# First pair of an attention kernel: one-hot and maximum rows transposed to the operands' own partitions, first head in column thirds, a planner with per-engine latencies

## The chip, the cores and the metric

The kernel runs on one core of one Trainium2 chip. The metric is device microseconds of one execution: before the change the median of three runs is 796.49 us (795.05, 796.49 and 796.76). A change of less than 0.2% (1.6 us) can't be told from none with such a measurement.

## What is computed

Clustered attention, then two feed-forward layers, all in float32:

```python
q_assign = argmax(einsum('bhsd,hcd->bhsc', q_n, c_n))   # k_assign likewise, 16 clusters
mask = q_assign[:, :, :, None] == k_assign[:, :, None, :]
scores = where(mask, scale * q @ k.T, -1e9)
attn = softmax(scores);  x = attn @ v                    # b=2, h=8, s=768, d=64
h = x @ moe_w_in;  x = (max(h,0) + alpha*min(h,0)) @ moe_w_out      # 1536x512, d_ff 2048
h = x @ moe2_w_in; x = (P(h)/Q(h)) @ moe2_w_out          # P cubic, Q from |h| and h*h
```

## The kernel before

**Precision.** Each float32 operand is split into a high part and the rest, and a product is three matmuls (high·high, high·low, low·high). The weights arrive as 64-bit words, and ScalarE, VectorE and GpSimd decode them (L992 to L1012) before a feed-forward step can use them.

**Attention, by pairs of heads.** There are 8 pairs (16 heads), and per pair j these steps: `load` brings q and k (L450); `ph_T` transposes them (L520, L522 for pair 0, L525 for the others) and splits them (L530, L532); `ph_logits` multiplies by the centroids (L552); `ph_lt` transposes the logits (L566) and makes a one-hot row of the best cluster in five VectorE instructions (L574 to L580); `ph_oht` transposes the one-hot of both heads at once (L590) and ScalarE scales it (L594).

**Operands.** `operands1(i)` copies to head i's operand `op1` with DMAs: q and k (L617), the one-hot of k's clusters (L620) and that of q's as 0 or -2^60 (L623). They have to be DMAs, since the rows go to other partitions than those on which they were made. `operands2(i)` copies the low parts to `op2` (L632, L636).

**Scores.** `max_chunk` multiplies `op1` by itself (L664), 9 chunks of 512 columns a head, and VectorE reduces each to row maxima (L670). `m_chain` collects them (L678), transposes them on TensorE (L684), ScalarE negates them (L686), and a DMA puts them as one more row into `op1` (L690). Only then can `st_chunk` make the scores minus the maximum (L709, L710) in 9 chunks; ScalarE takes the exponential (L714), the result is split into 16-bit high and low parts (`p_split`: L414/L416 and L726), and `pv_tile` multiplies by v (L773, L775; L787 to L789). `pv_fin` divides (L804 to L812), and `x_T` transposes for the feed-forward (L826).

**Feed-forward.** 96 steps of 512 columns; each is 12 matmuls of `emit_h` (L1029) and 12 of `emit_y` (L1098), with an activation between that runs on the other engines.

**Warm-up.** 57 operations of two small matmuls each (L848) with a low priority fill TensorE where it has nothing else.

**What sets the order.** All steps are operations of a planner, `Sched`. It has a cost for each operation and engine, keeps a modelled time for each engine, takes the operation that it can start first (weighted by a due time `SC.t`), and at the end writes the instructions of each engine in the order of their modelled starts. So a changed number changes the order on all engines, and the chip then executes each engine's list strictly in that order, with semaphores between them. All transfers stand in one list, SP's. The model of before takes a transfer's bytes at 280 GB/s and one latency of 0.16 us between any two engines:

```python
    LAT = 0.16
...
                moved = max(moved, start + 1.28) + cost
                o.end = moved + 1.05
...
        return n / 280e3
```

## Time and profile before

| what | value |
|---|---|
| median of three runs | 796.49 us |
| the profiled execution | 797.74 us, its span 796.0 us, 1.74 us around it |
| busy share of the span | TensorE 96%, VectorE 75%, ScalarE 70%, GpSimd 73% |
| mean granted clock of TensorE | 0.984 |
| attention, until the first feed-forward matmul | 252.09 us |
| first scores of head 0 (L709) | at 29.88 us |
| dense feed-forward | from about 277 us to 787 us |

The profile's page gives busy times, the chain of waits that ended last, and the costliest groups; the trace answers with a timeline of each engine, the waits of an engine by what released it, and the busy time in chosen windows with the granted clock. "SPq" is the issue of a transfer. A matmul's duration overlaps that of the next, so TensorE's rate is read from the distance of starts, not from durations.

### The profile page before, as it was taken

To read this page: it belongs to the slowest core of one execution; us is meant where nothing else is said; L and a number is where in the kernel's file an instruction comes from. 1 tells how busy PE (TensorE), PEld (TensorE's weight loads), DVE (VectorE), ACT (ScalarE), POOL (GpSimd) and SP (SyncE) were. 2 spreads that over 40 slices of the span, in tenths; PEclk is the share of its full clock that TensorE was granted. 3 is DMA by queue.
4 is the path that set the end of the run, shared out by engine and by line. 5 is a ranking of instruction groups with operands and counts; after the bars stand their busy time and mean duration, and the time that the engine had idled before them with its cause. 6 is when DMAs were issued, how large, how long until landed. Compare 5 with 4: busy or idle time off the path is not lost.

```text
span 796.0 us, 13977 instructions
## 1 busy us (share of the span) xinstructions
PE 765.4 (96%) x5295; PEld 636.0 (80%) x5295; DVE 599.4 (75%) x871; ACT 560.3 (70%) x991; POOL 579.7 (73%) x475
## 2 busy tenths in 40 slices
PE   8998999999997799999999999999999999999996
PEld 7687797887886688888888888888888888888885
DVE  5787787888797999775662563479889899777775
ACT  3377877887878666665653664688899798666672
POOL 4286956967679899996762773799889689667443
PEclk9899999999899999999999999999999999999999
DMA  5685757656442433332320330211112110000012
GB/s 129 127 171 115 156 126 151 136 123 175 97 102 81 159 99 114 107 108 77 107 80 0 106 96 11 79 54 54 53 54 80 53 54 1 0 1 1 1 54 106
DMA packets 57859, 67.58 MB, mean 85 GB/s; under 512 B 27232, under 2 KB 46272, under 8 KB 57792
## 3 DMA queue, kind: packets, MB, share of 16 engines
q1 hardware_dynamic: 57792, 66.69, 31.9%
q8 instruction: 41, 0.67, 0.4%
q14 instruction: 26, 0.21, 0.1%
HBM read 43.04 MB, written 3.15 MB: 58 GB/s over the span
## 4 chain that ended last, share of the span: by engine, by line
PE 84%; DVE 6%; DMA 5%; ACT 2%; POOL 1%; issue 1%; SPq 1%; DVEq 0%; ACTq 0%; POOLq 0%
PE bank L1029 32%; PE bank L1098 32%; PE bank L709 3%; PE bank L664 3%; PE bank L710 3%; DMA arena_r<-arena_r 2%; PE bank L787 2%; PE bank L552 2%; DVE mp L670 2%; PE bank L789 2%; PE bank L788 2%; DMA arena_p<-in_v 2%; PE bank L525 1%; DMA arena_p<-in_k 1%; DVE arena_p L726 1%
## 5 line engine op out<-in xcount | busy, mean ns | idle before, releaser
L1029 PE MATMUL bank<-x,arena_r 128*128 128x512 f32 x1152 | 277.6, 390 | 3.2 <-ACT arena_r L414 1.1
L1098 PE MATMUL bank<-arena_r 128*128 128x512 f32 x1152 | 277.8, 390 | 1.7 <-ACT arena_r L414 1.0
L1029 PEld LDWEIGHTS bank<-x,arena_r 128*128 128x128 f32 x1152 | 215.9, 188 | 48.9 <-POOL arena_r L1012 3.1
L1098 PEld LDWEIGHTS bank<-arena_r 128*128 128x128 f32 x1152 | 215.6, 188 | 48.4 <-ACT arena_r L414 1.4
L1075 POOL TENSOR_TENSOR arena_r<-arena_p,arena_r 128x512 fp32r<-128x512 f32 x96 | 132.9, 1385 | 38.6 <-ACT arena_r L414 19.8
L726 POOL TENSOR_TENSOR arena_p<-arena_p 128x768 f16<-128x768 f32 x66 | 115.3, 1755 | 18.7 <-ACT arena_p L414 15.1
L414 ACT CAST arena_r<-arena_p 128x512 fp32r<-128x512 f32 x137 | 83.4, 621 | 44.7 <-DVE arena_p L1040 28.1
L1005 POOL TENSOR_TENSOR arena_p<-arena_p 128x512 int32<-128x512 int32 x64 | 93.8, 1468 | 27.1 <-ACT arena_p L998 15.9
L670 DVE TENSOR_REDUCE mp<-bank 128x1 f32<-128x512 f32 x144 | 91.3, 683 | 16.8 <-PE bank L664 16.6
L1012 POOL TENSOR_TENSOR arena_r<-arena_p,arena_r 128x512 fp32r<-128x512 f32 x64 | 92.5, 1447 | 13.0 <-ACT arena_r L414 12.5
L714 ACT ACTIVATE arena_p<-bank 128x512 f32<-128x512 f32 x144 | 80.0, 593 | 30.3 <-PE bank L710 24.4
L1000 DVE TENSOR_SCALAR arena_p<-arena_p 128x512 uint32<-128x512 uint32 x64 | 64.3, 1004 | 38.7 <-ACT arena_p L992 38.7
L1040 DVE SCALAR_TENSOR_TENSOR arena_p<-arena_p,nal 128x512 f32<-128x512 f32 x48 | 53.0, 1106 | 50.2 <-ACT arena_p L1043 50.1
L1002 DVE SCALAR_TENSOR_TENSOR arena_p<-arena_p 128x512 uint32<-128x512 uint32 x64 | 84.1, 1315 | 1.5
L1057 POOL TENSOR_TENSOR arena_p<-arena_p 128x512 f32<-128x512 f32 x48 | 62.4, 1301 | 29.7 <-ACT arena_p L1054 29.5
L709 PE MATMUL bank<-arena_r 128*128 128x512 f32 x192 | 69.8, 381 | 1.4 <-DVE x L834 1.0
L1040 DVE SCALAR_TENSOR_TENSOR arena_p<-arena_p,cq,bank 128x512 f32<-128x512 f32 x48 | 35.7, 744 | 41.8 <-ACT bank L1065 36.1
L789 PE MATMUL bank<-arena_p 128*128 128x65 f16 x576 | 62.2, 197 | 3.6 <-POOL arena_p L726 2.9
L710 PE MATMUL bank<-arena_r 128*128 128x512 f32 x192 | 64.4, 349 | 0.0
L787 PE MATMUL bank<-arena_p 128*128 128x65 f16 x576 | 62.8, 197 | 0.0
L788 PE MATMUL bank<-arena_p 128*128 128x64 f16 x576 | 62.2, 195 | 0.0
L664 PE MATMUL bank<-arena_r 96*128 96x512 f32 x192 | 53.1, 372 | 7.9 <-DMA arena_r<-arena_r 3.5
(122 smaller groups left out, 1272.3 us busy)
## 6 DMA issues: line engine op xcount, KB each, us to landing
arena_p<-in_moe_w_in SPq DMA_DIRECT2D x32, 512.0 KB, 3.8
arena_p<-in_moe_w_out SPq DMA_DIRECT2D x32, 512.0 KB, 3.6
arena_r<-arena_r SPq DMA_DIRECT2D x24, 384.0 KB, 5.4
arena_r<-arena_r SPq DMA_DIRECT2D x24, 192.0 KB, 5.2
arena_p<-in_q SPq DMA_DIRECT2D x8, 384.0 KB
...
```

What stands on the lines that cost most here:

```text
L414: e.copy(o_, i_)
L670: op(dvep(CH), lambda e: e.reduce_max(mp.v[:, n0:n0 + 2 * np_ - 1:2], ps.v.rearrange("p (a k) -> p a k", a=np_), axis=AX.X), r=[ps], w=[(m ...
L709: e.matmul(o_, lhsT=b_.v[:, 1, ks], rhs=b_.v[:, 0, lo:hi], start=True, stop=False)
L710: e.matmul(o_, lhsT=a.v[:, 1, ks], rhs=a.v[:, 0, lo:hi], start=False, stop=True)
L726: lambda e: e.tensor_sub(pt_.v[:, 1, :], src(), pt_.v[:, 0, :]),
L1002: op(dve2(N), lambda e, d0=d0, hi=hi: e.scalar_tensor_tensor(u(d0), hi(), 0x80000000, u(d0), op0=ALU.bitwise_and, op1=ALU.bitwise_or), r=[ ...
L1005: op(pool2(N), lambda e, d0=d0, d1=d1: e.tensor_tensor(n32(d0), n32(d0), n32(d1), op=ALU.add), r=[d0, d1], w=[d0])
L1012: lambda e, wt=wt, pick=pick, src=src: e.tensor_tensor(pick(wt.v)[:, 1], src(), f32(pick(wt.v)[:, 0]), op=ALU.subtract),
L1029: e.matmul(ps.v, lhsT=wi.v[:, wi_, kk, :], rhs=x[kk][:, xi, cols], start=n == 0, stop=n == 3 * KD - 1)
L1040: lambda e: e.scalar_tensor_tensor(o_.v, a_.v, sc, b_.v, op0=p0, op1=p1))
L1075: op([dve2(N), pool2(N)], lambda e: e.tensor_tensor(gg.v[:, 1, :], G.v, f32(gg.v[:, 0, :]), op=ALU.subtract), r=[G, (gg, 0)], w=[(gg, 1)])
L1098: e.matmul(ps.v, lhsT=lhsT, rhs=rhs, start=first and wi_ == gi == 0, stop=last and gi == 1)
```

## The change

Six things are changed.

1. For pair 0, `first_masks` makes the one-hot in two halves, head by head, into one tile that has 64 zero columns ahead. `first_rows` transposes 80 columns at a time (24 transposes instead of 6), so that the 16 one-hot rows come out on partitions 64 to 79, where `op1` needs them. ScalarE or VectorE writes them from PSUM straight into `op1`. The four DMAs of L620 and L623 for heads 0 and 1 go away.
2. For head 0, `m_first` does the same with the maximum: two of the six query blocks at a time, transposed so that they land on partition 96, and written straight into `op1`. The DMA of L690 for head 0 goes away.
3. Head 0's scores are made in thirds of the columns (`st_first`, 256 columns), each as soon as its maximum is there; its split is in pieces of 256.
4. The last head's exponential stays in PSUM, and its split is read from there by ScalarE and VectorE; GpSimd has no part in it.
5. k of pair 1 is loaded at once, v of pair 0 earlier.
6. The planner has a tail for each producing engine and a semaphore latency for each waiting one, 190 GB/s for transfers, a gate for large ones, and other due times.

The core of the diff:

```diff
-WP = 0.0025
+WP = 0.0027
+GATE, BIGDMA = 0.9027, 0.3
...
-    LAT = 0.16
+    TAIL = {PE: 0.16, ACT: 0.1, DVE: 0.08, POOL: 0.04, DMA: 0.0}
+    SEM = {PE: 0.14, ACT: 0.04, DVE: 0.04, POOL: 0.08, DMA: 0.03}
...
+                    if e == DMA and cost_ > BIGDMA:
+                        st = max(st, moved - 1.2 - GATE)
...
-                moved = max(moved, start + 1.28) + cost
-                o.end = moved + 1.05
+                moved = max(moved, start + 1.2) + cost
+                o.end = moved + 0.69
...
-    EARLY = 77.8906
+    EARLY = 92.9972
+    W0, W1, VE = 135.3459, -3.0098, 53.7153
+    LATE0, LATE1, FK1, FV0, FO1, HALF = 0.0, 20.0, 4.5, 17.9752, 12.0, 8.0
...
-        return n / 280e3
+        return n / 190e3
...
+    def first_rows():
+        for e_ in range(2):
+            SC.t += HALF * e_
+            for sd, nm, (sc_, bi_) in ((0, "oh", (1.0, 0.0)), (1, "neg", (BIG, -BIG))):
+                ps, a = SC.buf("S", "ph1"), op1[e_]
+                def tr(e, ps=ps, e_=e_, sd=sd):
+                    pb = ps.v.bitcast(BF16)
+                    for t in range(T):
+                        g = (2 * t + sd) * C
+                        e.transpose(pb[:D + C, t * P:(t + 1) * P], moh.v[:, e_, g:g + D + C], idb)
+                op((PE, 0.34), tr, r=[(moh, e_)], w=[ps])
+                op([act_p(S), but(dvep(S), 0.05 - BIAS["DVE"])], lambda e, ps=ps, a=a, sd=sd, sc_=sc_, bi_=bi_: (
+                    e.activation(a.v[D:D + C, 1 - sd, :], ps.v.bitcast(BF16)[D:D + C, :S],
+                                 ACTF.Copy, scale=sc_, bias=bi_) if e is nc.scalar else
...
+    def m_first(u):
+        mp, a, ps = maxparts[0], op1[0], SC.buf("o", "m0")
...
+        op((DVE, 0.09), lambda e: e.reduce_max(
+            mz.v[:, two], mp.v[:, 6 * u:6 * u + 6].rearrange("p (t a) -> p t a", a=3), axis=AX.X),
+           r=[(mp, c) for c in range(3 * u, 3 * u + 3)], w=[(mz, u)])
+        def tr(e):
+            for k_ in range(2):
+                at = 2 * u + k_
+                e.transpose(ps.v[:97, k_ * P:(k_ + 1) * P], mz.v[:, at:at + 97], idf)
...
+        row = lambda: a.v[96:97, 0, 2 * u * P:(2 * u + 2) * P]
+        op([act_p(2 * P), dvep(2 * P)], lambda e: (
+            e.activation(row(), ps.v[96:97, :2 * P], ACTF.Copy, scale=-1.0, bias=LNP / scale)
...
+        if i >= LASTS:
...
+            op(act_p(CH), lambda e: e.activation(ps.v, ps.v, ACTF.Exp, scale=scale),
+               r=[ps], w=[ps])
...
+                op([act_p(hi - lo), dvep(hi - lo)],
+                   lambda e, t_=t_, src=src, lo=lo, hi=hi: copy(e, t_.v[:, 0, lo:hi], src()),
+                   r=[ps], w=[(t_, 0, lo)])
+                op(dvep(hi - lo), lambda e, t_=t_, src=src, lo=lo, hi=hi: e.tensor_sub(
+                    t_.v[:, 1, lo:hi], src(), t_.v[:, 0, lo:hi]),
+                   r=[ps, (t_, 0, lo)], w=[(t_, 1, lo)])
...
-    STEP = 5.2
+    STEP = 5.2741
...
-            SC.t = T0 + STEP * (s - 8.5752)
+            SC.t = T0 + STEP * (s - 4.2479)
```

Two places show what this does to the order. The first is VectorE's list at the first head. Before, from the end of pair 0's one-hot (L580) over the rest of pair 1's split (L532) and the nine reductions of head 0 (L670, `mp_114`) to the row maximum (L678):

```order
L580 TENSOR_TENSOR arena_p<-arena_p,lmw_109 128x384
L532 TENSOR_TENSOR x<-bank,x 128x256 x2
L532 TENSOR_TENSOR x<-bank,x 128x512
L670 TENSOR_REDUCE mp_114<-bank 128x1
L670 TENSOR_REDUCE mp_114<-bank 128x2
L670 TENSOR_REDUCE mp_114<-bank 128x1 x2
L670 TENSOR_REDUCE mp_114<-bank 128x2
L670 TENSOR_REDUCE mp_114<-bank 128x1 x2
L670 TENSOR_REDUCE mp_114<-bank 128x2
L670 TENSOR_REDUCE mp_114<-bank 128x1
L678 TENSOR_REDUCE mx_111<-mp_114 128x6
```

Now the same stretch, with its new lines (L620 is the one-hot's last step, L539 pair 1's split, L641 one copy of a transposed one-hot into `op1`, L739 the reductions, L770 the maximum of two query blocks, L425 a high part of head 0's split):

```order
L620 TENSOR_TENSOR arena_p<-arena_p,lmw_109 128x192 x2
L539 TENSOR_TENSOR x<-bank,x 128x256
L539 TENSOR_TENSOR x<-bank,x 128x512
L641 TENSOR_SCALAR arena_r<-bank 16x768
L739 TENSOR_REDUCE mp_114<-bank 128x1
L739 TENSOR_REDUCE mp_114<-bank 128x2
L739 TENSOR_REDUCE mp_114<-bank 128x1 x2
L770 TENSOR_REDUCE arena_p<-mp_114 128x2
L739 TENSOR_REDUCE mp_114<-bank 128x2
L739 TENSOR_REDUCE mp_114<-bank 128x1 x2
L770 TENSOR_REDUCE arena_p<-mp_114 128x2
L739 TENSOR_REDUCE mp_114<-bank 128x2
```

A copy into `op1` has come between the one-hot and the reductions, and the maximum of the first two query blocks stands after four reductions instead of nine.

The second is SP's list around the operands of head 6, the seventh of the 16. Before (L617 is q and k of `op1`, L620 and L623 its one-hot rows, L632 and L636 `op2`, L690 a maximum row):

```order
L617 DMA arena_r<-arena_r 64x1536
L632 DMA arena_r<-arena_r 64x2x768
L620 DMA arena_r<-arena_r 16x768
L623 DMA arena_r<-arena_r 16x768
L636 DMA arena_r<-arena_r 64x768 x2
L690 DMA arena_r<-arena_r 1x6x128
```

Now (the same transfers are L684, L701, L689, L692, L705 and L759, and L457 loads v):

```order
L684 DMA arena_r<-arena_r 64x1536
L689 DMA arena_r<-arena_r 16x768
L692 DMA arena_r<-arena_r 16x768
L457 DMA arena_p<-in_v 128x2x384
L701 DMA arena_r<-arena_r 64x2x768
L705 DMA arena_r<-arena_r 64x768
L759 DMA arena_r<-arena_r 1x6x128
```

All three transfers that the maxima of head 6 need now stand ahead of the large ones of `op2`.

More of the change, by code (lines that the diff above doesn't have):

```diff
@@ L209, in run @@
                     ready.append(x)
+                if raw is None:
+                    x.est = max(x.est, o.start)
+                    continue
+                lat = self.TAIL[eng] + self.SEM[x.alts[0][0]]
+                x.est = max(x.est, o.end + lat) if len(x.alts) > 1 or x.alts[0][0] != eng else max(
+                    x.est, o.end + (self.SAME if raw and eng != PE else 0.0))
             order.append(o)
@@ L698, in st_chunk @@
+    p32s, pkeys = {}, {}
+    LASTS = NHEAD - 1
     def st_chunk(i, c):
@@ L700, in st_chunk @@
         u, cc = divmod(c, CPU)
-        if cc == 0:
+        if cc == 0 and i < LASTS:
             p32s[i, u] = SC.buf("p32")
-        p32, parts = p32s[i, u], pieces(cc)
+        p32, parts = p32s.get((i, u)), pieces(cc)
         def mm(e):
```

166 lines of the change are left out of this document (130 added, 36 removed).

## The prediction

> **What bounds the kernel now.** I read the page first, then the busy time in windows with the granted clock, then the timeline of the start, then TensorE's waits. From the page come the span, TensorE's share and the clock that the throttle granted in 40 slices:
>
> ```profile
> span 796.0 us, 13977 instructions
> PE 765.4 (96%) x5295; PEld 636.0 (80%) x5295; DVE 599.4 (75%) x871; ACT 560.3 (70%) x991; POOL 579.7 (73%) x475
> PEclk9899999999899999999999999999999999999999
> ```
>
> TensorE leads, but its 96% is a mean over stages. The windows (length, then busy time of TensorE, its weight loads, VectorE, ScalarE and GpSimd, the clock, the transfers' share and GB/s) separate them:
>
> ```profile
> 0.00:30.00 30.00, 25.20 (x218) 21.07 (x218) 19.48 (x50) 8.34 (x17) 9.34 (x36) 0.99 0.58 128
> 60.00:240.00 180.00, 170.36 (x2234) 146.13 (x2232) 146.57 (x275) 143.12 (x277) 130.25 (x106) 0.97 0.59 130
> 240.00:281.00 41.00, 32.04 (x372) 25.60 (x369) 37.09 (x40) 31.90 (x58) 37.13 (x25) 0.96 0.35 116
> 281.00:776.00 495.00, 495.00 (x2184) 409.15 (x2183) 362.09 (x452) 348.86 (x587) 375.23 (x285) 1.00 0.18 58
> 776.00:796.00 20.00, 13.97 (x61) 10.91 (x59) 11.49 (x18) 5.74 (x9) 7.04 (x6) 0.95 0.29 105
> ```
>
> From 281 to 776 us TensorE has no idle time and a full clock, and the change takes no matmul out of there: nothing is to be had. What is to be had lies in the start, in 180 - 170.4 = 9.6 us of idle time (and a clock of 0.97) in the middle, in 9 us at the hand-over to the feed-forward, and in the tail.
>
> **The start.** The timeline (start, duration, engine, line) shows a chain of latencies. I quote the first operand transfer, the first and last step of pair 0's one-hot, its transposes, the scaling, the last transfer of a one-hot row, the maxima, head 0's maximum row and the first scores:
>
> ```profile
> 9.36 0.65 SPq L617 DMA_DIRECT2D arena_r<-x  x1
> 12.26 0.56 DVE L574 TENSOR_REDUCE lmx<-bank 128x24 f32<-128x384 f32 x1 [0.71 <-PE bank L566]
> 14.42 0.56 DVE L580 TENSOR_TENSOR arena_p<-arena_p,lmw 128x384 bf16<-128x384 bf16 x1
> 15.04 0.52 PE L590 MATMUL bank<-idb,arena_p 128*64 128x128 bf16 x6
> 15.66 0.99 ACT L594 ACTIVATE arena_r<-bank,osc 64x768 fp32r<-64x768 bf16 x1 [3.88 <-PE bank L590]
> 18.64 0.59 SPq L623 DMA_DIRECT2D arena_r<-arena_r  x1
> 20.63 2.36 PE L664 MATMUL bank<-arena_r 96*128 96x512 f32 x9
> 21.15 5.47 DVE L670 TENSOR_REDUCE mp<-bank 128x1 f32<-128x512 f32 x9 [1.65 <-PE bank L664]
> 27.62 0.84 SPq L690 DMA_DIRECT2D arena_r<-arena_r  x1
> 29.88 0.79 PE L709 MATMUL bank<-arena_r 128*128 128x512 f32 x1 [0.33 <-DVE mp L670]
> 37.71 0.27 PE L684 MATMUL bank<-idf,mx 128*6 128x128 f32 x1
> ```
>
> The last row is the maximum of head 1, the point at which both heads' 18 reductions are over. VectorE's costs there, by groups (count, busy time, mean ns), and the window in which nothing but operands is moved (190 GB/s):
>
> ```profile
> L670 DVE TENSOR_REDUCE mp<-bank 128x1 f32<-128x512 f32 x23 | 15.4, 684 | 2.3 <-PE bank L664 2.3
> L532 DVE TENSOR_TENSOR x<-bank,x 128x512 fp32r<-128x512 f32 x4 | 2.8, 689 | 1.3 <-ACT x L530 1.2
> L759 DVE TENSOR_TENSOR arena_p<-bank,arena_p 128x384 f16<-128x384 f32 x2 | 1.1, 558 | 0.3 <-ACT arena_p L414 0.3
> L678 DVE TENSOR_REDUCE mx<-mp 128x6 f32<-128x18 f32 x3 | 0.5, 172 | 0.1
> 20.50:26.50 6.00, 5.78 (x35) 3.82 (x33) 5.35 (x9) 0.72 (x2) 0.00 (x0) 1.00 0.98 190
> ```
>
> **The change, part by part.**
>
> *Step 1, the first scores.* The one-hot becomes ten instructions of half the length. Halved in proportion they cost what the five of before did (12.26 to 14.98 us, 2.7 us); if each keeps a fixed part, up to 0.7 more. I take 3.0: done at 15.3. The 24 transposes cost 4 x 0.52 = 2.1 at most, the first half of them about 1, then come copies of 768 columns (L594: 0.99), two engines sharing them, and on VectorE the rest of pair 1's split (about 1.2) ahead of its copy: the first maxima at about 17.4 instead of 20.63. Four reductions (2.7), a maximum (0.17), two transposes and a copy (0.3 each, with waits 0.9): the row is there at 21.5. The scores also need `op2`. SP's list now has `op1` of heads 0 and 1, half of `op2`, `op1` of head 2 and the other half of `op2` in a row: five times 393 KB, 2.07 us each at 190 GB/s. A one-hot row (49 KB, 0.26 us) takes 20.63 - 18.64 = 2.0 us from issue to use, 1.7 of it latency; so 9.36 + 1.7 + 10.35 = 21.4. Both arrive together, and the first scores start 8.4 us earlier than at 29.88.
>
> *Step 2, what of it is kept.* VectorE is the limit behind that. From the end of the one-hot to head 1's maximum it now has 18 reductions (12.3), pair 1's split (1.2), a copy of one-hot rows (0.95), three small maxima (0.5), four pieces of head 0's split (1.0), pair 1's one-hot (2.6, as before), v's split (1.1) and small ones (0.4): 20.0 us, against 12.3 + 1.3 + 2.6 + 0.3 = 16.5 before. It ends at 15.3 + 20.0 + 0.4 of waits = 35.7, head 1's maximum is transposed at 36.0 instead of 37.71: 1.7 us. By then TensorE has done all of head 0's scores and 18 matmuls of P·v, some 0.9 us of work that it did later before. So 8.4 us turn into 2.6.
>
> *Step 3, the middle.* TensorE's waits from 38 to 240 us (in total, times, longest):
>
> ```profile
> PE bank L664 <- DMA arena_r<-arena_r: 3.5, 3, 1.8
> PE bank L552 <- DMA arena_r<-x: 2.0, 1, 2.0
> PE bank L684 <- DVE arena_p L575: 1.7, 1, 1.7
> PE bank L664 <- ACT arena_r L530: 1.6, 1, 1.6
> ```
>
> The longest of the first row is head 6, whose one-hot rows are issued behind a large transfer of `op2`:
>
> ```profile
> 89.16 0.50 SPq L617 DMA_DIRECT2D arena_r<-arena_r  x1
> 89.69 0.63 SPq L632 DMA_DIRECT2D arena_r<-arena_r  x1
> 91.82 1.61 SPq L623 DMA_DIRECT2D arena_r<-arena_r  x1
> 97.24 1.31 PE L664 MATMUL bank<-arena_r 96*128 96x512 f32 x4 [1.78 <-DMA arena_r<-arena_r]
> 97.61:101.02 3.41, 3.41 (x30) 3.10 (x29) 1.89 (x3) 0.55 (x2) 2.74 (x2) 0.50 0.00 0
> 200.01:206.83 6.82, 6.82 (x63) 6.24 (x59) 5.05 (x11) 5.54 (x12) 3.56 (x4) 0.50 0.00 0
> ```
>
> The planner of before took 280 GB/s where the trace has 190, so it thought that these rows would be there in time. The new order puts them first. The three waits are worth 3.5 us. The last two rows show half the clock right behind a wait of 1.78 (and of 1.69 before 200): 3.41 us at half speed lose 1.7 more, which go with the wait of head 6. The other waits stay in my sum. On the other side a new order brings new waits: nothing if all is well, at most what the old order has (9.6); I take 1.5, one wait nearly as long as the longest of the last rows of the table (1.6).
>
> The Trainium skill (TensorE: Matmul & The Clock Gate, Part 1) says that the clock falls to half after an idle window of about 3.4 us; by that, waits of 1.8 us cost no clock and the total would come out 1.7 later. The trace disagrees: half the clock follows pauses of 1.78 and 1.69 us.
>
> *Step 4, the hand-over.* TensorE waits there for the last head's split and for decoded weights; the groups of 240 to 281 us give the prices:
>
> ```profile
> PE bank L789 <- POOL arena_p L726: 2.9, 1, 2.9
> L1002 DVE SCALAR_TENSOR_TENSOR arena_p<-arena_p 128x512 uint32<-128x512 uint32 x8 | 12.0, 1504 | 0.2
> L1000 DVE TENSOR_SCALAR arena_p<-arena_p 128x512 uint32<-128x512 uint32 x8 | 11.2, 1396 | 0.0
> L726 POOL TENSOR_TENSOR arena_p<-arena_p 128x768 f16<-128x768 f32 x5 | 9.9, 1971 | 0.0
> L726 DVE TENSOR_TENSOR arena_p<-arena_p 128x768 f16<-128x768 f32 x5 | 5.6, 1129 | 0.0
> ```
>
> The last head's low parts leave GpSimd and come to VectorE: nine chunks of about 0.7 (L532's kind) are 6.4 us, and I count 5 x 1.5 + 4 x 1.4 of decoding between the ends of the last two heads but one, against 6 x 1.5 + 6 x 1.4 and four L726 (4.5) before: with the rest about 24 us then and now. So the 2.9 goes, but the weights are 1.5 tiles later, and the third feed-forward step waits for them. I take 1 us gained; the bounds are 5 (all waits of this stage halved) and -4 (one and a half tiles, each 1.4 + 1.5 on VectorE).
>
> *Step 5, the tail.* The last step waits 0.99 us:
>
> ```profile
> 787.95 3.02 PE L1098 MATMUL bank<-arena_r 128*128 128x512 f32 x12 [0.99 <-ACT arena_r L414]
> ```
>
> The new order starts the last step's ScalarE work ahead of the previous step's exponential: 0.3 gained, between 1.0 gained (the whole wait) and as much lost, since GpSimd now copies the last step but one behind the last step's product. k of pair 1 loaded early moves while the queue has nothing else and costs nothing; were it late, the whole start would shift by its 1.4 us.
>
> Sum: -2.6 - 3.5 - 1.7 + 1.5 - 1.0 - 0.3 = -7.6 us. The profiled execution took 797.74 (span 796.0 and 1.74 around it), 1.25 over the median of 796.49; so 790.1 on its scale and 788.9 as a median.
>
> **The rivals.** (a) *The early scores are kept whole.* If VectorE isn't the limit at the start and 8.4 us stay, and the clock is full there: -7.6 - 5.8 = 783.1. For it: VectorE is busy only 19.48 of the first 30 us. Against: the sum of step 2. (b) *Nothing arrives.* The start's 2.6 are taken up where TensorE is bound later, and the new order's waits equal the old: 796.5, within 0.2%. For it: nearly the same matmuls stand in nearly the same order from 60 to 240 us. (c) *Slower, by the clock.* Between the first and second third of head 0 the new list has 40 small warm-up matmuls, so TensorE has gaps there, and every head's hand-over is a candidate. Each further window of 3.41 us at half speed costs 1.7; five of them eat the 7.6, and eight give 796.49 - 7.6 + 13.6 = 802.5. A mean clock of 0.984 is 796 x 0.016 / 0.5 = 25 us at half speed now, about seven such windows, so their number would have to double. (d) *The rows still go by DMA:* excluded by the order, in which the four one-hot transfers of the first pair are missing.
>
> **How the numbers follow.** Forecast (with its bounds) 0.55, (a) 0.20, (b) 0.13, (c) 0.12. A measurement here can't tell less than 0.2%, 1.6 us. The forecast's own range is 784 to 794: the bounds of steps 4 and 5 and of the new waits. With (a) and half of (b) the range is 781 to 796. Faster by over 0.2%: 0.55 + 0.20 and a little of (b), 0.78; within: 0.10; slower: 0.12.
>
> **What would show it.** Right: first scores of head 0 near 21.5 us and head 1's maximum transposed near 36; no wait of the maxima for a transfer over 0.5 us between 60 and 240; half the clock in at most five windows; TensorE's wait for the last head's split shorter than 2.9 and one for weights behind it. Wrong: first scores after 25 us; waits of 1.7 us with half the clock behind them at new places; dense feed-forward later than 277 us.

## The result, and the profile after

The changed kernel takes 772.07 us (median of four runs, 771.58 to 773.19) where the kernel before, on the same chip, takes 795.77 (794.75 to 796.76). The ratio is 0.9704, 95% interval 0.9686 to 0.9723: faster by 3.0%. I had forecast 788.9 with a range of 781 to 796. The sign was right, the size was a third of what came.

The page of the changed kernel shows a span shorter by 25.5 us, TensorE at 98% instead of 96%, and a granted clock that is 9 from end to end:

```profile
span 770.5 us, 14098 instructions
PE 756.6 (98%) x5330; PEld 633.8 (82%) x5330; DVE 600.7 (78%) x893; ACT 552.4 (72%) x990; POOL 595.1 (77%) x506
...
PEclk9999999999999999999999999999999999999999
```

The windows by stage tell where it went. First the kernel before, now cut at its own stages (60 us, the last head's first scores at 232, the dense feed-forward, which has no idle time, from 280):

```profile
0.00:60.00 60.00, 54.03 (x456) 44.23 (x457) 42.15 (x90) 30.66 (x62) 30.07 (x56) 0.91 0.69 143
60.00:232.00 172.00, 162.36 (x2113) 139.44 (x2110) 140.68 (x264) 135.15 (x263) 122.87 (x100) 0.97 0.58 128
232.00:280.00 48.00, 39.04 (x485) 31.45 (x484) 41.98 (x53) 39.01 (x70) 43.51 (x29) 0.96 0.41 127
```

Then the changed kernel, whose last head begins at 216 and whose dense feed-forward begins by 256:

```profile
0.00:60.00 60.00, 55.02 (x548) 48.08 (x549) 46.94 (x115) 35.04 (x76) 35.68 (x75) 0.95 0.71 149
60.00:216.00 156.00, 154.63 (x2061) 134.97 (x2059) 132.32 (x253) 139.96 (x269) 122.34 (x94) 1.00 0.65 141
216.00:256.00 40.00, 38.72 (x491) 32.11 (x491) 37.93 (x60) 35.13 (x70) 33.94 (x25) 1.00 0.47 140
256.00:746.00 490.00, 490.00 (x2159) 404.37 (x2158) 369.98 (x447) 333.95 (x565) 393.71 (x305) 1.00 0.19 59
746.00:770.50 24.50, 18.20 (x79) 14.24 (x77) 13.50 (x21) 8.37 (x13) 9.47 (x9) 0.94 0.24 87
```

Length less TensorE's busy time is its idle time: 6.0, 9.6 and 9.0 us before, 5.0, 1.4 and 1.3 now. The middle and the hand-over have almost none left. The second part of the account is the clock. A stretch at half clock costs half of TensorE's busy time in it. Taken from the exact stretches of the granted clock that is 11.4 us before (windows of 3.41 or 6.83 us that begin at 29.3, 43.0, 97.6, 200.0 and 264.9 us) and 3.1 us now (one stretch, 54.0 to 60.9). What remains when both are taken off is TensorE's work at full clock, 754.0 us before and 753.5 now: the work is the same to 0.5 us, and the gain is 16.6 us of idle time (the last steps, 6.0 us before and 6.3 now, counted in) and 8.3 us of clock.

The start, answering to the rows of before: the first and last step of pair 0's one-hot, the first maxima, the first scores and head 1's maximum:

```profile
13.77 0.61 DVE L611 TENSOR_REDUCE lmx<-bank 128x12 f32<-128x192 f32 x2
...
15.69 0.62 DVE L620 TENSOR_TENSOR arena_p<-arena_p,lmw 128x192 bf16<-128x192 bf16 x2
...
18.55 1.77 PE L733 MATMUL bank<-arena_r 96*128 96x512 f32 x7
...
23.09 0.36 PE L806 MATMUL bank<-arena_r 128*128 128x256 f32 x1 [0.16 <-issue]
...
35.67 0.27 PE L753 MATMUL bank<-idf,mx 128*6 128x128 f32 x1
```

TensorE's waits from 38 to 216 us (in total, times, longest). These are all that the view lists there; the first two lie at the start of the stretch, at 54 and 52 us:

```profile
PE bank L532 <- DMA arena_p<-in_q: 0.9, 1, 0.9
PE bank L573 <- ACT arena_p L421: 0.7, 1, 0.7
PE bank L733 <- issue: 0.5, 1, 0.5
PE bank L532 <- DMA arena_p<-in_k: 0.4, 1, 0.4
PE bank L733 <- DVE mp L739: 0.4, 1, 0.4
PE bank L733 <- DMA arena_r<-arena_r: 0.3, 1, 0.3
```

The maxima (L733, before L664) waited 3.5 us for transfers; now it is 0.3. And the waits that I had left in the sum (2.0 of the logits, 1.7 of the maximum's transpose, 1.6 for a split) are gone as well.

The hand-over: VectorE's groups from 216 to 256 us (count, busy time, mean ns):

```profile
L1162 DVE SCALAR_TENSOR_TENSOR arena_p<-arena_p 128x512 uint32<-128x512 uint32 x8 | 8.3, 1053 | 0.1
L1160 DVE TENSOR_SCALAR arena_p<-arena_p 128x512 uint32<-128x512 uint32 x8 | 8.1, 1028 | 0.2 <-ACT arena_p L1152 0.2
L857 DVE TENSOR_TENSOR arena_p<-bank,arena_p 128x512 f16<-128x512 f32 x6 | 4.1, 690 | 0.4 <-ACT arena_p L421 0.2
...
L857 DVE TENSOR_TENSOR arena_p<-bank,arena_p 128x256 f16<-128x256 f32 x6 | 2.3, 416 | 0.0
```

The last head's low parts (L857) take 4.1 + 2.3 = 6.4 us, as I had counted. The two decoding steps (L1160, L1162; before L1000, L1002) take 1.03 and 1.05 us each where I had counted 1.4 and 1.5, and no wait of TensorE in this stretch is longer than 0.4 us.

### The profile page after: what moved, and what is told of

Same layout as the page of the kernel before. It is cut to its first block, busy times and chain, and to the rows that moved or that the text cites. A ratio compares the mean times of both kernels' runs of the same rounds, so it can differ in the third digit from the quotient of the medians.

```text
span 770.5 us, 14098 instructions
## 1 busy us (share of the span) xinstructions
PE 756.6 (98%) x5330; PEld 633.8 (82%) x5330; DVE 600.7 (78%) x893; ACT 552.4 (72%) x990; POOL 595.1 (77%) x506
## 4 chain that ended last, share of the span: by engine, by line
PE 54%; DVE 16%; ACT 12%; POOL 12%; issue 3%; DMA 2%; SPq 1%; DVEq 0%; POOLq 0%; ACTq 0%
PE bank L1258 16%; PE bank L1189 16%; DVE arena_p L1200 6%; PE bank L733 4%; PE bank L840 4%; PE bank L841 3%; POOL arena_p L1217 3%; DVE arena_p L1277 3%; DVE bank L1200 2%; POOL arena_r L1235 2%; ACT arena_p L1223 2%; ACT bank L1225 2%; POOL arena_r L1172 2%; PE bank L559 2%; PE bank L938 2%
## 5 line engine op out<-in xcount | busy, mean ns | idle before, releaser
L1258 PE MATMUL bank<-arena_r 128*128 128x512 f32 x1152 | 278.3, 390 | 1.3 <-POOL arena_r L423 0.9
L1235 POOL TENSOR_TENSOR arena_r<-arena_p,arena_r 128x512 fp32r<-128x512 f32 x96 | 136.5, 1423 | 35.4 <-ACT arena_r L421 30.6
L876 POOL TENSOR_TENSOR arena_p<-arena_p 128x768 f16<-128x768 f32 x62 | 108.9, 1764 | 22.7 <-ACT arena_p L421 15.6
L1200 DVE SCALAR_TENSOR_TENSOR arena_p<-arena_p,nal 128x512 f32<-128x512 f32 x48 | 57.5, 1197 | 56.1 <-ACT arena_p L1203 55.7
L421 ACT CAST arena_r<-arena_p 128x512 fp32r<-128x512 f32 x119 | 72.1, 622 | 38.1 <-DVE arena_p L1200 26.7
L1172 POOL TENSOR_TENSOR arena_r<-arena_p,arena_r 128x512 fp32r<-128x512 f32 x64 | 95.8, 1502 | 1.8 <-ACT arena_r L421 0.4
L739 DVE TENSOR_REDUCE mp<-bank 128x1 f32<-128x512 f32 x144 | 91.0, 681 | 7.0 <-PE bank L733 6.6
L1162 DVE SCALAR_TENSOR_TENSOR arena_p<-arena_p 128x512 uint32<-128x512 uint32 x64 | 82.0, 1282 | 1.4
L1160 DVE TENSOR_SCALAR arena_p<-arena_p 128x512 uint32<-128x512 uint32 x64 | 65.9, 1031 | 20.7 <-ACT arena_p L1152 20.5
L862 ACT ACTIVATE arena_p<-bank 128x512 f32<-128x512 f32 x126 | 69.7, 594 | 11.6 <-PE bank L841 8.4
L1200 DVE SCALAR_TENSOR_TENSOR arena_p<-arena_p,cq,bank 128x512 f32<-128x512 f32 x48 | 35.8, 746 | 41.3 <-ACT bank L1225 34.9
L840 PE MATMUL bank<-arena_r 128*128 128x512 f32 (+1 forms) x180 | 63.2, 365 | 0.4 <-ACT bank L849 0.3
L1223 ACT ACTIVATE arena_p<-arena_p,cq 128x512 f32<-128x512 f32 x48 | 34.8, 726 | 40.1 <-POOL arena_p L1217 39.7
L1202 ACT ACTIVATE arena_p<-bank 128x512 f32<-128x512 f32 x48 | 28.8, 599 | 47.5 <-PE bank L1189 47.5
L938 PE MATMUL bank<-arena_p 128*128 128x65 f16 x576 | 61.6, 195 | 0.0
L940 PE MATMUL bank<-arena_p 128*128 128x65 f16 x576 | 60.9, 195 | 0.0
```

What stands on the lines that cost most here:

```text
L739: op(dvep(CH), lambda e: e.reduce_max(mp.v[:, n0:n0 + 2 * np_ - 1:2], ps.v.rearrange("p (a k) -> p a k", a=np_), axis=AX.X), r=[ps], w=[(m ...
L840: e.matmul(o_, lhsT=b_.v[:, 1, ks], rhs=b_.v[:, 0, lo:hi], start=True, stop=False)
L876: lambda e: e.tensor_sub(pt_.v[:, 1, :], src(), pt_.v[:, 0, :]),
L938: e.matmul(o1, lhsT=hi, rhs=d.v[:, e_, kt, 64:129], start=kt == 0, stop=False)
L1162: op(dve2(N), lambda e, d0=d0, hi=hi: e.scalar_tensor_tensor(u(d0), hi(), 0x80000000, u(d0), op0=ALU.bitwise_and, op1=ALU.bitwise_or), r=[ ...
L1172: lambda e, wt=wt, pick=pick, src=src: e.tensor_tensor(pick(wt.v)[:, 1], src(), f32(pick(wt.v)[:, 0]), op=ALU.subtract),
```

## The experiments

Three theories were set against each other. **M**: the truer planner model takes the waits out of the middle, whatever stands at the start. **N**: the tuned due times are a lucky find, and neighbours of this order would be as slow as the old one. **S**: the shorter start and the last head's path carry the gain. All profiles are put in one account, made as above: TensorE's idle time in three stages (up to 60 us; from there to the last head's first scores; from there to the fourth feed-forward step), half of its busy time at half clock, and the rest, its work at full clock. The idle time of the last steps, 5.8 to 7.0 us in all of them, is left out of the columns. The ratio is to runs of the kernel before on the same chip. The changed kernel's own two ratios, from two chips, lie 0.3% apart, so a difference of that size between rows of different chips shows nothing.

| kernel | median us | ratio (95%) | idle to 60 | middle | hand-over | clock | work |
|---|---|---|---|---|---|---|---|
| before | 795.77 | 1 | 6.0 | 9.6 | 9.0 | 11.4 | 754.0 |
| changed | 772.07 | 0.9704 (0.9686–0.9723) | 5.0 | 1.4 | 1.3 | 3.1 | 753.5 |
| a_oldmodel | 792.52 | 0.9994 (0.9977–1.0011) | 9.9 | 4.5 | 7.3 | 6.8 | 755.2 |
| b_newmodel | 786.75 | 0.9918 (0.9900–0.9937) | 4.9 | 0.4 | 9.4 | 9.3 | 752.8 |
| b_newdma | 794.61 | 0.9992 (0.9976–1.0008) | 5.4 | 7.0 | 9.4 | 12.3 | 752.9 |
| b_newsem | 804.48 | 1.0116 (1.0086–1.0145) | 5.8 | 11.4 | 10.2 | 13.2 | 754.9 |
| b_jit1 | 798.78 | 1.0042 (1.0022–1.0063) | 6.0 | 13.7 | 4.9 | 14.3 | 752.7 |
| b_lastonly | 789.45 | 0.9929 (0.9911–0.9948) | 6.7 | 8.8 | 5.1 | 4.9 | 756.1 |
| b_newmodel_last | 778.07 | 0.9789 (0.9766–0.9811) | 5.0 | 0.4 | 4.5 | 4.9 | 753.7 |
| b_nml_ffn | 778.00 | 0.9782 (0.9749–0.9814) | 4.7 | 0.2 | 3.2 | 6.4 | 754.1 |
| a_lastoff | 782.63 | 0.9859 (0.9835–0.9884) | 5.5 | 1.6 | 6.9 | 6.6 | 753.9 |
| a_jit1 | 777.64 | 0.9798 (0.9781–0.9815) | 5.1 | 0.7 | 6.5 | 4.9 | 752.8 |
| a_ffnold | 773.08 | 0.9720 (0.9693–0.9747) | 5.5 | 1.7 | 1.3 | 2.8 | 753.3 |
| a_nofirst | 793.69 | 0.9980 (0.9961–1.0000) | 7.2 | 6.8 | 7.4 | 8.1 | 754.9 |
| a_nofirst2 | 777.86 | 0.9781 (0.9762–0.9800) | 5.1 | 1.8 | 3.6 | 8.1 | 751.6 |
| a_swap6 | 773.20 | 0.9734 (0.9708–0.9759) | 4.9 | 2.8 | 1.4 | 2.9 | 752.6 |
| a_swapall | 779.89 | 0.9802 (0.9772–0.9833) | 6.6 | 6.1 | 1.3 | 3.8 | 754.9 |
| a_params | 774.51 | 0.9740 (0.9721–0.9760) | 7.8 | 1.4 | 1.3 | 2.8 | 753.0 |
| a_params2 | 767.55 | 0.9679 (0.9663–0.9694) | 4.2 | 2.0 | 1.2 | 0.0 | 753.6 |
| changed, again | 772.13 | 0.9736 (0.9723–0.9750) | 4.9 | 1.3 | 1.3 | 1.5 | 753.4 |

The last column stays between 751.6 and 756.1 in all twenty profiles while the times go from 767 to 804. So TensorE's work is the same to within these 4.5 us, and a larger difference has to be read in the four columns before it.

### The planner's model

**a_oldmodel**: the changed kernel, all of it but the planner's model, which is that of before.

```diff
-    TAIL = {PE: 0.16, ACT: 0.1, DVE: 0.08, POOL: 0.04, DMA: 0.0}
-    SEM = {PE: 0.14, ACT: 0.04, DVE: 0.04, POOL: 0.08, DMA: 0.03}
+    LAT = 0.16
...
-                moved = max(moved, start + 1.2) + cost
-                o.end = moved + 0.69
+                moved = max(moved, start + 1.28) + cost
+                o.end = moved + 1.05
...
-        return n / 190e3
+        return n / 280e3
```

> The new kernel with the planner's model of before (280 GB/s, one latency of 0.16 us, no gate), all else new. Theory M (the truer model takes the waits out of the middle): TensorE's idle time between 60 us and the hand-over comes back, 1.4 -> 8 to 12 us, with half the clock in 2 to 4 windows; 782 to 788 us. Theory N (the new due times do it): the due times are kept, so 772 to 776. Theory S (the shorter start and the last head's path do it): 772 to 776.

It took 792.52 us: with the old model the new start, the last head's path and the due times, taken together, are worth nothing (0.9994). N and S, which had 772 to 776, fall in this form. M's numbers were not met either: it had 8 to 12 us of idle time in the middle and 782 to 788 us, and the middle has 4.5 while idle time is back in every stage. This run alone can't tell a bad model from due times that were written for another one; the runs on the kernel before, which keep the old due times, can.

**b_newmodel**: the reverse, the kernel before with the new model alone.

> The kernel before with the new planner model alone (190 GB/s, tails and semaphore latencies by engine, the gate), its structure and due times kept. Theory M: most of the middle is gained, 9.6 us of idle time down to 2 to 4 and at most one window of half the clock between 60 and 240 us: 782 to 787 us. Theory N (old due times don't suit, the model alone is worth little): 793 to 800. Theory S: 794 to 797.

The middle is nearly empty, with the old start, old due times and a first score at 30.0 us. The window of the stage and the largest wait of the hand-over:

```profile
60.00:215.00 155.00, 154.63 (x2103) 134.30 (x2102) 139.90 (x259) 133.56 (x260) 118.13 (x95) 1.00 0.63 139
```

```profile
PE bank L793 <- DVE arena_p L730: 2.8, 1, 2.8
```

Its last head begins at 215.0 us, as early as in the changed kernel (215.8), but the hand-over keeps 9.4 us of idle time, the largest wait for the last head's split, and 786.75 us is all that comes of it. So M holds for the middle and not for the hand-over.

**b_newdma** and **b_newsem** split the model: the first has only the transfers' part (190 GB/s, their two latencies, the gate, and one price for all loads of q and k, where the model of before counted those of pairs 1 to 7 double, 2.8 us instead of 2.07), the second only the latencies between engines (TAIL, SEM and their bookkeeping).

> The kernel before with one half of the new model: transfers at 190 GB/s, their two latencies and the gate for large ones; the latencies between engines stay as before. If the rate of transfers is what empties the middle (the step of my prediction that counted three waits), idle time from 60 us to the last head falls under 2 us (9.6 before, 0.4 with the whole model) and the last head starts near 215 to 217. If the latencies between engines do it, idle time stays over 5 us and the last head comes after 224.

> The kernel before with the other half of the new model: a tail for each producing engine and a semaphore latency for each waiting one; transfers stay at 280 GB/s. If the rate of transfers is what empties the middle, idle time there stays over 5 us with waits for transfers of one-hot rows, and the last head comes after 224. If the latencies between engines do it, idle time falls under 2.5 us.

Neither empties the middle. TensorE's waits from 60 us on, first with the transfers' part:

```profile
PE bank L569 <- DVE arena_p L815: 2.9, 1, 2.9
PE bank L792 <- DVE arena_p L729: 1.2, 1, 1.2
...
PE bank L667 <- DMA arena_r<-arena_r: 0.3, 1, 0.3
```

then with the latencies' part:

```profile
PE bank L665 <- DMA arena_r<-arena_r: 5.7, 3, 2.1
PE bank L665 <- ACT arena_p L415: 2.2, 1, 2.2
```

The transfers' part removes the waits that I had counted (3.5 to 0.3 us), but waits for VectorE come in their place and the time stays (0.9992). With the latencies' part alone the transfers' waits grow to 5.7 and the kernel is slower by 1.2%. Only both together bring the middle to 0.4. My either-or was wrong: neither part does it by itself.

**b_jit1** moves two due times of the kernel before by about 1% (AHEAD 14.0 to 13.85, one offset -5.1427 to -5.2).

> The kernel before, its old model kept, with two of its due numbers moved by about 1% (14.0 to 13.85, -5.1427 to -5.2). It shows how far the order alone scatters under the old model. If the old model is what leaves waits in the middle, idle time there stays over 4 us and the time between 790 and 802. If the changed kernel's order is just a lucky one of many, the time can come out anywhere, also under 785, with idle time in the middle under 2.5.

798.78 us, with 13.7 us idle in the middle. Six kernels have the old model or half of the new one: they have 4.5 to 13.7 us there. Of the kernels with the whole new model and SP's list left alone, eight have 0.2 to 1.8, and one, a_nofirst, has 6.8.

### The start

**a_nofirst**: the changed kernel with pair 0's rows and head 0's maximum by DMA again and whole chunks for head 0 (items 1 to 3 of the change undone).

> The changed kernel without the new start: pair 0's one-hot and head 0's maximum go through DMAs again and head 0's scores are made in whole chunks; the planner's model, its due times and the last head's path stay new. Theory M (the truer model makes the middle's gain, so the start's lead is swallowed by it): first scores near 30 us, but TensorE's idle time in the middle stays under 2.5 us and the last head comes no more than 2 us later than in the changed kernel; 772 to 775 if the hand-over keeps its order, up to 781 if it falls back as it did with the moved due times. Theory S (the start's lead is kept to the end): 779 to 781 with all of the loss before 60 us. Told apart by the time at which the last head's first scores start (215.8 us in the changed kernel).

793.69 us. Neither M nor S had that. From 100 to 227 us this kernel is as full as the changed one (126.41 us busy of 127), and what it loses ahead of the hand-over lies from 38 to 100 us: 62 - 53.39 = 8.6 us idle there (the next expectation gives 10.7 for it). The hand-over, with 7.4 instead of 1.3, and the clock, with 8.1 instead of 3.1, make most of the rest. The due times had been written for the other start. **a_nofirst2** gives the old start its own numbers back:

```diff
-    EARLY = 92.9972
+    EARLY = 77.8906
-    W0, W1, VE = 135.3459, -3.0098, 53.7153
+    W0, W1, VE = 135.3459, -3.0098, 0.0
-    LATE0, LATE1, FK1, FV0, FO1, HALF = 0.0, 20.0, 4.5, 17.9752, 12.0, 8.0
+    LATE0, LATE1, FK1, FV0, FO1, HALF = 18.6, 27.0, 9.0, 27.2, 0.0, 8.0
```

> The changed kernel without its new start, as in the run that took 793.69, but now the due times and release times that were written for the new start go back to those of before (EARLY 77.8906, LATE0 18.6, LATE1 27.0, FK1 9.0, FV0 27.2, FO1 0, VE 0); all others stay new. If that run was slow because these numbers didn't fit its start, idle time from 38 to 100 us falls from 10.7 to under 3 us and the time to 771 to 779. If the new start itself is what makes the middle run through, the time stays over 785.

Here are the two kernels in the same windows, first with the numbers for the other start:

```profile
38.00:100.00 62.00, 53.39 (x645) 43.98 (x644) 47.39 (x84) 43.89 (x88) 37.81 (x33) 0.95 0.66 134
100.00:227.00 127.00, 126.41 (x1662) 109.47 (x1660) 108.75 (x207) 112.47 (x215) 97.48 (x79) 1.00 0.62 137
```

and with its own:

```profile
38.00:100.00 62.00, 59.33 (x709) 50.00 (x709) 51.99 (x93) 50.78 (x100) 43.52 (x39) 0.94 0.70 142
100.00:218.00 118.00, 117.07 (x1601) 103.47 (x1600) 101.31 (x198) 108.57 (x210) 89.17 (x72) 1.00 0.63 140
```

Idle time from 38 to 100 us falls from 8.6 to 2.7, that of the hand-over from 7.4 to 3.6, and the time to 777.86. Two things follow. A due time belongs to one structure; moved to another these cost 15.8 us. And against the changed kernel (0.9704 and 0.9736) this ratio of 0.9781 makes the new start worth 0.45 to 0.77%, 3.6 to 6.1 us. The account shows it mostly as clock: 8.1 us lost against 3.1 and 1.5, all of it before 50 us. b_nml_ffn below, which has the old start with the numbers written for it, has nearly the same ratio, 0.9782.

### The hand-over

**a_lastoff**: the changed kernel with the last head's split as before, which is one line, `LASTS = NHEAD`.

> The new kernel with the last head split as before (through SBUF, low parts on GpSimd and VectorE). Theory S (this path is the hand-over's gain, because VectorE's decoding slows from 1.03 and 1.05 us to 1.4 and 1.5 when GpSimd subtracts beside it): 777 to 781 us, the idle time at the hand-over 1.3 -> 6 to 9 us. Theory M (the hand-over is gained by the better order): 772 to 774.

782.63 us; idle time at the hand-over 6.9 instead of 1.3 us, and the last P·v at 254.2 instead of 243.5. The split runs on SBUF again, and VectorE's share of it is dear:

```profile
L876 DVE TENSOR_TENSOR arena_p<-arena_p 128x768 f16<-128x768 f32 x7 | 11.1, 1601 | 0.2 <-ACT arena_p L421 0.2
```

**b_newmodel_last** and **b_lastonly** put this path into the kernel before, with the new model and with the old.

> The kernel before with the new planner model and with the last head's split from PSUM, but with its old start and its old due times. With the model alone it took 786.75 and kept 9.4 us of idle time at the hand-over. If the last head's path is what empties the hand-over, its idle time falls under 4 us and the time to 777 to 781. If the path needs the tuned due times too (as the run with the moved due times suggests), idle time there stays over 6 us and the time over 783.

> The kernel before with the last head's split from PSUM alone; the planner's old model, the old start and the old due times stay. With the new model as well, the last head's path took 8.7 us off (786.75 to 778.07). If the path is worth that by itself, 785 to 789, with idle time at the hand-over under 5 us (9.0 before). If it needs the order of the new model, 791 to 799.

With the new model 778.07 us, by itself 789.45. In ratios: the model alone takes 0.8% off, the path alone 0.7%, both 2.1%, so that 0.6% (some 5 us) would come only of the two together. That isn't shown: two moved due times alone change as much (0.4% in b_jit1, 0.6 to 0.9 in a_jit1 below), and in the account of the profiles the two simply add up. From before, idle time and clock fall by 12.0 us with the model, by 10.5 with the path and by 21.2 with both. The path alone still has 8.8 us idle in the middle, 4.8 of them waits of maxima for transfers. **b_nml_ffn** adds the feed-forward's three due numbers to the first of them, **a_ffnold** takes them out of the changed kernel, and **a_jit1** moves two other due times of the changed kernel by about 1% (AHEAD 14.9599 to 14.8, -4.6204 to -4.7).

```diff
-    STEP = 5.2
+    STEP = 5.2741
...
-        SC.t = T0 + STEP * (s - 0.0901)
+        SC.t = T0 + STEP * (s - -0.0819)
...
-            SC.t = T0 + STEP * (s - 8.5752)
+            SC.t = T0 + STEP * (s - 4.2479)
```

> The kernel before with the new planner model, the last head's path and, in addition, the three new due numbers of the feed-forward steps; its start and all other due numbers stay as they were. Without the feed-forward numbers it took 778.07 with 4.5 us of idle time at the hand-over, its last head as early (214.8 us) as that of the changed kernel (215.8). If the start's lead is swallowed and the feed-forward numbers make the rest, this kernel comes to 771.5 to 774 with idle time at the hand-over under 2 us, though its first scores still start at 29.9. If the new start is worth something to the end, it stays at 775 to 778.

> The changed kernel with the feed-forward's due numbers of before; the order before 220 us stays nearly the same. If these numbers make what is left of the hand-over, its idle time rises from 1.3 to about 4.5 us and the time to 775 to 778. If they are idle numbers, the time stays within 1.5 us of 772.

> The new kernel with two due times moved slightly (AHEAD 14.96 -> 14.8, the maxima's -4.62 -> -4.7). Theory M: the order stays good, 771 to 775 us. Theory N (the numbers are a lucky find): 776 to 784, waits come back at some heads.

The feed-forward's numbers are idle: 778.00 with them and 778.07 without, 773.08 without them and 772.07 with. Two small moves elsewhere (a ratio of 0.9798) cost 0.6 to 0.9% against the changed kernel's two ratios, and the idle time shows where: 1.3 to 6.5 us at the hand-over, while the middle stays empty (0.7). The longest wait of the moved order there:

```profile
PE bank L1258 <- ACT arena_r L421: 3.2, 1, 3.2
```

The copy that ended this wait had itself waited for the step's activation (L1200), which VectorE reached only after two decoding steps of 1.20 and 1.64 us:

```profile
254.80 0.62 ACT L421 CAST arena_r<-arena_p 128x512 fp32r<-128x512 f32 x1 [0.98 <-DVE arena_p L1200]
```

So N has a part after all: the middle comes with the model, but the last 5 us of the hand-over depend on the order. One neighbour keeps them (a_ffnold, 1.3 us idle), another loses them (a_jit1).

### One late transfer, and the clock

**a_swapall** and **a_swap6** leave every engine's list as it is and move in SP's list alone the first transfer of a head's low parts ahead of the next head's one-hot rows, at ten heads (the expectations count eleven) and at head 6 alone. This is the arrangement to which my third step put down its 3.5 + 1.7 us.

> The changed kernel with the same order on every engine, but in SP's list the first transfer of a head's low parts stands ahead of the next head's one-hot rows for eleven of the heads, as it did for head 6 before the change. If the place in SP's list decides (the step of my prediction that gives each such wait 1.2 to 1.8 us and half the clock behind it), TensorE gets waits of maxima for transfers of 1 to 2 us each at several heads, windows of half clock behind them, and the time rises by 4 to 20 us. If the lead of the maxima over their use in the new order covers a transfer of 2.07 us, the waits stay under 0.5 us and the time within 1.5 us of 772.

> The changed kernel with one transfer moved in SP's list: the low parts of head 5 stand ahead of the one-hot rows of head 6, as before the change; every other engine has the same list. With the same at eleven heads there was one wait of 1.95 us for head 6 with 3.41 us of half clock behind it. If one late transfer has this price at this place, the wait comes again (1.5 to 2.0 us), half clock behind it, and the time is 774.5 to 777. If the wait came of a queue that was already late from earlier heads, it stays under 0.5 us and the time within 1.5 us of 772.

With all ten the time is 779.89 us and the middle has 6.1 us of idle time. Two heads wait for rows, the longest at head 6, and half clock follows:

```profile
94.17 0.95 PE L739 MATMUL bank<-arena_r 96*128 96x512 f32 x4 [1.95 <-DMA arena_r<-arena_r]
```

```profile
92.55:95.97 3.42, 1.80 (x24) 1.58 (x25) 1.29 (x2) 2.08 (x5) 3.14 (x4) 1.00 0.75 218
95.97:99.38 3.41, 3.41 (x28) 2.85 (x26) 3.41 (x5) 2.42 (x5) 0.65 (x1) 0.50 0.03 7
```

With head 6 alone its wait is there again, 1.52 us, but the clock stays:

```profile
90.82 0.93 PE L739 MATMUL bank<-arena_r 96*128 96x512 f32 x4 [1.52 <-DMA arena_r<-arena_r]
```

```profile
86.59:90.01 3.42, 2.71 (x46) 2.14 (x44) 1.84 (x6) 3.38 (x8) 2.81 (x4) 1.00 0.52 122
90.01:93.42 3.41, 2.60 (x30) 2.30 (x31) 2.09 (x3) 1.89 (x5) 3.22 (x3) 1.00 0.86 232
93.42:96.83 3.41, 3.41 (x65) 3.04 (x64) 3.23 (x7) 2.97 (x7) 2.28 (x2) 1.00 0.02 7
```

The time of a_swap6, 773.20, can't be told from the changed kernel's. I had expected half clock there, and that was wrong. The mechanism of a late transfer is real; its price, as far as these two runs tell, depends on where the pause lies in the windows of 3.41 us in which the clock changes. The pause of 1.95 falls into one window, which is then busy for 1.80 us of 3.42; the pause of 1.52 is shared by two, busy for 2.71 and 2.60.

**a_params** and **a_params2** go for the one stretch at half clock that the changed kernel has left. TensorE's pauses before it end with a load of q that is late by 0.87 us. Ahead of it SP spent 3.56 us on issuing a small parameter load:

```profile
41.71 3.56 SPq L1107 DMA_DIRECT2D nca<-in_moe_a  x1
```

```profile
54.21 1.11 PE L532 MATMUL bank<-idf,arena_p 128*128 128x128 f32 x4 [0.87 <-DMA arena_p<-in_q]
```

```profile
50.61:54.03 3.42, 1.99 (x12) 1.12 (x10) 2.57 (x5) 3.20 (x9) 1.71 (x2) 1.00 1.00 182
54.03:57.44 3.41, 2.79 (x12) 2.31 (x13) 1.67 (x4) 1.05 (x3) 3.27 (x3) 0.50 1.01 202
```

The first kernel moves q and k of pair 3 ahead of the three small loads, the second moves the small loads to a place where SP waits for 10.7 us (22.5 to 33.3 us). All other engines keep their lists. The edit of the second:

```diff
+        oh2 = self.mark["oh", 2].start
+        for n in range(3):
+            self.mark["par", n].start = oh2 - 1e-6 * (3 - n)
         order.sort(key=lambda o: (o.start, o.prio))
```

> The changed kernel with the loads of q and k of pair 3 moved ahead of three small parameter loads and a load of v in SP's list; all other engines keep their lists. The issue of one of these small loads took 3.56 us on SP, and TensorE then waited 0.87 us for q at 54.21 us, at the end of a window of 3.41 us in which it was busy for only 1.99, and had half the clock for the next 6.83 us. If the late load causes the pause and the pause the half clock, the wait goes, and 1 to 4.5 us with it: 767.5 to 771. If the half clock has another cause (the wait for ScalarE just before it, or no pause at all), at most 1 us goes: 771 to 772.5.

> The changed kernel with the three small parameter loads moved the other way: in SP's list they now stand ahead of the one-hot rows of head 2, where SP waits for 10.7 us (22.5 to 33.3 us) in the changed kernel. All other engines keep their lists. The run before moved them back, and then ScalarE and GpSimd, which use them, stood in wait (6.15 and 2.01 us), so that a new pause of 4.2 us took the place of the old one. If the late load of q makes TensorE's pause at 54 us and the pause its half clock, both go now: idle time up to 60 us falls from 5.0 to 4 or less, the half clock behind 54 us is gone, and the time is 767 to 770.5. If the pause stays (the wait for ScalarE of 0.74 us and other gaps of that window are enough for the half clock), 770.5 to 772.5.

> The changed kernel once more, on the same chip and beside the same runs of before, so that the run with the moved parameter loads has its reference: 771.5 to 773.5, with half the clock behind the pause at 54 us again.

The first took 774.51 us, for a reason that I had not looked for: the small loads came so late that ScalarE, which uses one of them, stood waiting with all that is queued behind it, and TensorE with it.

```profile
ACT bab L1118 <- DMA bab<-in_moe_b: 6.1, 1, 6.1
```

```profile
55.73 0.79 PE L736 MATMUL bank<-arena_r 96*128 96x512 f32 x1 [4.22 <-ACT arena_p L865]
```

The second took 767.55 us, and the changed kernel beside it 772.13. The load still takes SP 3.79 us, but where nothing waits. The window is now busy for 2.72 us, and no stretch at half clock is left in the whole kernel:

```profile
23.58 3.79 SPq L1111 DMA_DIRECT2D nca<-in_moe_a  x1
```

```profile
50.12:53.53 3.41, 2.72 (x19) 1.88 (x18) 3.41 (x7) 2.68 (x7) 2.83 (x5) 1.00 0.54 108
53.53:56.94 3.41, 3.38 (x83) 3.25 (x82) 3.26 (x9) 1.50 (x4) 2.83 (x4) 1.00 0.67 136
```

This is the version that is faster than both kernels: a ratio of 0.9679 (0.9663 to 0.9694) against 0.9736 (0.9723 to 0.9750) on the same chip, for three entries of one list. Idle time up to 60 us fell to 4.2; I had said 4 or less. The two profiles account for only 1.4 us of the 4.6 between the medians, since the profiled execution took 770.56 us for the changed kernel and 769.23 for the new one. The granted clock points to the missing stretch: 0.994 or 0.995 in the four other executions of the changed kernel and 0.999 in the three others of this one. What makes the issue itself so long isn't shown: the load of two numbers behind it takes 0.43 us, and a transfer of low parts (L705, at 48.70 in the changed kernel) takes 4.76.

## Why the prediction was right in sign and wrong in size

Against the account of the two profiles, in us:

| step | predicted | measured | of it idle time, clock |
|---|---|---|---|
| start (steps 1, 2) | -2.6 | -3.2 | -1.0, -2.2 |
| middle (step 3) | -3.5 - 1.7 + 1.5 = -3.7 | -12.9 | -8.2, -4.7 |
| hand-over (step 4) | -1.0 | -9.1 | -7.7, -1.4 |
| tail (step 5) | -0.3 | +0.3 | |
| work at full clock | 0 | -0.5 | |

**Steps 1 and 2 came out near their number, but in part by chance.** The first scores came at 23.09 us instead of 21.5: the one-hot took 2.5 us (I had 3.0), but it began at 13.77 instead of 12.26, since transposes of pair 1, whose k is now loaded at once, stand ahead of those of pair 0's logits on TensorE (which end at 13.66), and a part of its split ahead of the one-hot on VectorE. Head 1's maximum came at 35.67 (predicted 36.0). VectorE is busy for 17.85 of the 19.4 us from the one-hot's end to it, so it does limit this stretch, as step 2 had it; that the stretch was 1.0 us shorter than my sum and began 1.0 later cancelled. But the 37.71 with which step 2 compares was not set by VectorE. In the kernel before, VectorE had finished head 1's maximum at 34.54:

```profile
34.37 0.17 DVE L678 TENSOR_REDUCE mx<-mp 128x6 f32<-128x18 f32 x1
```

Its transpose stood behind head 0's scores on TensorE, which had half the clock from 29.3 to 36.2 us. So I read the gain at this point as mostly clock, though no run separates it; in the account 2.2 of the stage's 3.2 us are clock, a term that steps 1 and 2 had left out. Rival (a), the early scores kept whole, isn't borne out: the stage gained 3.2 us and not 8.4, and b_newmodel, with the old start, reaches the last head at 215.0 us, the changed kernel at 215.8. That the start is worth 3.6 to 6.1 us to the whole (a_nofirst2) is mostly clock as well.

**Step 3 failed, and it failed in one sentence: "The other waits stay in my sum."** Its mechanism was right. The one-hot rows do come in time in the new order, and putting head 6's behind a large transfer brings back a wait of 1.5 to 1.95 us. But I treated the planner's model as a repair of three places. It decides the whole list: with both parts of the new model nearly all waits of the middle go, those for VectorE and ScalarE as well (9.6 to 1.4 us), and with them the half clock behind 97.6 and 200 us, of which I had counted one window. The +1.5 for new waits fits a model that is only half right: b_newdma, which loses the three waits, gets 2.9 + 1.2 us of others for VectorE.

**Step 4 was mis-sized, and its new wait did not come.** I held the hand-over's lists to be as long as before and gave them 1.0 (bounds -4 to 5). The 6.4 us of low parts on VectorE were right. "The weights are 1.5 tiles later" was not: decoding took 1.03 + 1.05 us a tile instead of the 1.4 + 1.5 that I took from the old stage, and the feed-forward's first steps wait 0.4 us in all, for a copy on ScalarE. The runs split the gain: taking the last head's path away brings idle time from 1.3 to 6.9 in the new order, and decoding to 1.18 + 1.40 us (a_lastoff); moving two due times brings it to 6.5 (a_jit1). Why this order fits and that neighbour doesn't was not settled; I can only say where the neighbour waits.

**Step 5** had the size of a guess. The last wait moved to another step and is 0.86 instead of 0.99 us:

```profile
759.20 5.86 PE L1258 MATMUL bank<-arena_r 128*128 128x512 f32 x24 [0.86 <-POOL arena_r L423]
```

Rival (b), nothing arrives, described the kernels with the old model (a_oldmodel: 0.9994) and not this one. Rival (c), slower by the clock, was far off: instead of doubling, the stretches at half clock went from five ahead of the tail to one. My list of what would show the forecast wrong named only ways in which it could be too good.

## What to carry to other kernels

When a change corrects the model by which an order is planned, don't price it by the waits that it names; price it by all idle time of the stages that the order covers, and keep as a bound that all of it goes. Make the account of idle time, clock and work first: in the twenty profiles here it leaves a work that is the same to within 0.3% of the span to either side, and for the kernel before it shows 24.6 us of idle time and 11.4 of clock ahead of the last steps, where I had looked for 7.6. A transfer that is small in bytes is not small in its queue: look at what its issue takes, and move it to where the queue has nothing to do, never to where an engine that needs it has a long list behind.

## What the runs showed of the chip

**The clock changes in windows of 3.41 us, and a window that is too little busy costs the next.** Stretches at half clock lasted 3.41, 6.83 or 10.24 us. In the twenty profiles, from 60 to 745 us, I took all such windows at full clock, aligned to where the clock changed, and set two bounds afterwards to part them: of 20 with TensorE busy for less than about 45% of the window, all 20 were followed by half clock; of 24 between 45 and 62%, eight were; of some 3900 above 62%, none was. In the first 60 us, where many matmuls are short transposes, half clock also follows windows that are busy for 70 to 90%, so these bounds don't hold there. The Trainium skill (TensorE: Matmul & The Clock Gate, Part 1) has the clock fall after an idle window of about 3.4 us. The window's length agrees with the 3.41; that it must be idle does not: 1.80 us busy of 3.42 was enough. Why some windows between 45 and 62% pass and others don't stays open.

**VectorE's decoding depends on what GpSimd does.** Over the whole of the changed kernel, the durations of the first decoding step and of the last head's low parts (minimum, median, maximum in ns):

```profile
L1160 DVE TENSOR_SCALAR arena_p<-arena_p x64: 414/1017/1524, 182.3 to 659.9; 128x512 uint32<-128x512 uint32 x64
```

```profile
L857 DVE TENSOR_TENSOR arena_p<-bank,arena_p x12: 415/550/693, 227.7 to 239.4; 128x512 f16<-128x512 f32 x6, 128x256 f16<-128x256 f32 x6
```

Sorted by what GpSimd does meanwhile, the first has a median of 415 ns where it is idle (6 cases) and 1510 where it is busy all through (36 cases, 432 to 1524), the second decoding step (L1162) 690 (6) and 1666 (33, 850 to 1785). L857, which reads one input from PSUM, takes 681 to 693 ns for 512 columns in all six cases, though GpSimd is busy beside each for all or part of it. The Trainium skill (GPSIMD Engine Reference, Specifications) says that the two engines share SBUF interfaces and get in each other's way in VectorE's two-port modes or with two inputs from SBUF. The trace agrees for L1162, which has two inputs from SBUF, and for L857, which has one; in which mode L1160 runs, no trace here shows. So a price of VectorE's work must be taken with its neighbour. My 1.4 and 1.5 us were the price in a stage where GpSimd was busy for 0.88 and 0.79 of the decoding steps' time, now it is 0.72 and 0.69; the three first steps that had the last heads' subtraction (L726) on GpSimd beside them took 1.86 to 1.88 us.

**A lagging engine holds what stands behind it.** ScalarE stood for 6.15 us before a step of 0.20 us, and TensorE for 4.22, released by the exponential (L865) that ScalarE had behind that step (a_params). The Trainium skill (TensorE: Matmul & The Clock Gate, Part 1, on the array's architecture) says that ScalarE and VectorE take their queues strictly in order; the trace agrees for ScalarE.
